# The tail rows of four batches through the second channel product: two plain products, or one pair by the seven-product method

## The chip, the cores and the metric

The kernel runs on one core of one Trainium2 chip. The metric is the time of one execution in microseconds (us). A core has several engines, each with a program of its own that it works through in order: TensorE (PE) multiplies matrices, VectorE (DVE), ScalarE (ACT) and GpSimd (POOL) do the elementwise work, SyncE (SP) issues transfers (DMAs). They wait for one another by semaphores. PE reads its operands from the on-chip memory and writes its results into eight banks of 128 x 512 f32; the other engines read the results there.

## The reference

Eight batches of 576 rows. First an attention without softmax, then a normalization of each head, then a block with a product over the rows (token mix) and two products over the 512 features (channel products):

```python
kv  = np.einsum('bhsd,bhse->bhde', k, v)          # 8 heads of 64
out = np.einsum('bhsd,bhde->bhse', q, kv)
rms = np.sqrt(np.mean(out * out, axis=-1, keepdims=True) + 1e-06)
x   = out / rms * g_norm                           # -> [8, 576, 512]

a1  = alpha1 * x + beta1
tok = np.einsum('ts,bsd->btd', w_tok, a1)
u   = x + lam * tok
a2  = alpha2 * u + beta2
ch  = np.maximum(a2 @ w_ch1, 0.0) @ w_ch2          # 512 -> 2048 -> 512
return u + lam * ch
```

## The kernel before

**Tiles.** The 576 rows of a batch are four blocks of 128 (c = 0 to 3) and a tail of 64. The tails of two batches (0 and 1, 2 and 3, 4 and 5, 6 and 7) share one block of 128 rows. `xm` holds the rows of a batch, `xt` the tails; x, then u, then the result stand in the same place there. `xt` has two slots, for two pairs of batches in turn.

**Stages of a batch.** kv (L638, L644, f32 matmuls), the product with q and its norm (L729 on PE, L696 to L717 on ACT, DVE and POOL), the token mix (L812, for tails L857) with its add on DVE (L822), a cast to bf16 on POOL (L900) and a transposing DMA on SP (L913) into `a2m` (`a2l` for tails). Then the first channel product: L1090 with 16 blocks of 128 of the 2048 features, four matmuls of 512 columns each; for tails L1104, 128 columns (130 in batch 1, where two columns more give a bias, L1115). ACT applies the ReLU and writes `ht` for the four blocks, `hl` for the tails (L1112 for batches 0 and 1, L1121 later).

**Second channel product.** For batches 0 and 1 it is plain (`ch2`, L1151): 16 matmuls of 512 columns for each block of rows, and once more 16 for the tails of both (c = 4). From batch 2 on `strassen(b)` takes the four blocks as a 2 x 2 matrix of blocks, and the weights too (B11, B12, B21, B22), and forms the result from seven products (`product`, L1212, matmuls of 256 columns) in place of eight. It needs sums of blocks: of the weights once (`weight_sums`), of the activations per batch (`sums` ahead of the products, `sums_late` between them), all in `both` on DVE (L1174). Three products stay apart: ACT copies each (`keep`, L1242) and POOL adds it to the result (L1245). The other four results are added by DVE (`last_add`, L1250). SP stores them (L1263).

**The tails of batches 2 to 7.** Those of 2 and 3 go through `ch2_tail`: 16 matmuls for the left 256 columns (L1306), and 16 for the right half (L1312) against a sum that DVE makes in between; `finish` adds (L1327) and stores them (L1346). The tails of 4 to 7 are two blocks of 128 rows and go through the seven-product method as a pair, `strassen(NB)`, at the end of the program, after batches 6 and 7 (whose first channel products are formed together, L1031 and L972).

**What sets the order.** The code makes a list of operations with their reads and writes. `ORDER` is a string written out by hand with their numbers in the order in which every engine meets them; `:n` names the bank, `+` weaves the matmuls of two operations one by one, `~n` puts in n idle matmuls. `GATES` makes single operations wait for others. Semaphore waits follow from reads, writes and gates. POOL also issues the loads of K and V (L1465 the large ones, L1469 the 64 tail rows), SP the loads of q (L1457), all in the place where `ORDER` has them. A load of q is turned by DVE (L1475).

Of the kernel before, what the change touches and what calls it, by code (L numbers as in the profile page):

```python
# [13 lines left out]
NB = 8  # L14
# [344 lines left out]
def bass_transnormer_attn__then__resmlp_affine_kernel(  # L359
# [15 lines left out]
    with ExitStack() as stack:  # L375
# [843 lines left out]
        def strassen(b):  # L1219
# [58 lines left out]
            if tails:  # L1278
                store(0, fl)
# [343 lines left out]
```

## Time and profile before

| | us |
|---|---|
| median of 3 runs | 327.81 (327.43 to 328.18) |
| profiled execution | 328.12 |
| its span, first to last instruction | 326.3 |
| PE busy | 319.0 (98%) |
| DVE busy | 250.2 (77%) |
| ACT busy | 177.1 (54%) |
| POOL busy | 141.9 (43%) |

The span starts with the first instruction of the profiled execution, and all places in time are counted from there. In rows of a timeline the first number is the start, the second how long one instruction or a series took; `[... <-X]` is the time that the engine stood idle before it, and what released it. In rows by groups `| busy, mean ns of one | idle before, releaser`. A row of the chain of waits is the start, the length, and what worked. In tables by stage each row has a stretch, its length, the busy time of PE, PE's weight loads, DVE, ACT and POOL with the number of instructions in brackets, the granted clock, the DMA share and GB/s. DMA issues end with the time from issue to landing. Names of tiles are without their numbers: `w` is `w1` or `w2`, `ps` a result bank, `hh` the buffer that holds `ht` and `hl`.

### The profile page before, as it was taken

To read this page: it belongs to the slowest core of one execution; us is meant where nothing else is said; L and a number is where in the kernel's file an instruction comes from. 1 tells how busy PE (TensorE), PEld (TensorE's weight loads), DVE (VectorE), ACT (ScalarE), POOL (GpSimd) and SP (SyncE) were. 2 spreads that over 40 slices of the span, in tenths; PEclk is the share of its full clock that TensorE was granted. 3 is DMA by queue.
4 is the path that set the end of the run, shared out by engine and by line. 5 is a ranking of instruction groups with operands and counts; after the bars stand their busy time and mean duration, and the time that the engine had idled before them with its cause. 6 is when DMAs were issued, how large, how long until landed. Compare 5 with 4: busy or idle time off the path is not lost.

```text
span 326.3 us, 6145 instructions
## 1 busy us (share of the span) xinstructions
PE 319.0 (98%) x2411; PEld 218.2 (67%) x2441; DVE 250.2 (77%) x459; ACT 177.1 (54%) x363; POOL 141.9 (43%) x147
## 2 busy tenths in 40 slices
PE   8989999999999999999999999999999999999996
PEld 7767664454766545786579874787657644589884
DVE  4586078667799997838985388889899899997672
ACT  5684572329633471738741876731883068765520
POOL 3699127798362562353337143455234600014041
PEclk9999999999999999999999999999999999999999
DMA  7999997999950994799449950998040340000116
GB/s 258 316 267 257 214 243 176 224 151 209 265 123 16 204 245 70 173 247 217 104 50 186 259 104 11 213 253 171 2 129 2 64 145 4 0 2 2 64 50 209
DMA packets 108532, 48.15 MB, mean 148 GB/s; under 512 B 82061, under 2 KB 101717, under 8 KB 108504
## 3 DMA queue, kind: packets, MB, share of 16 engines
q0 software_dynamic: 26800, 21.38, 33.4%
q1 hardware_dynamic: 72240, 25.06, 33.4%
q10 hardware_dynamic: 9464, 1.32, 2.5%
q8 instruction: 19, 0.31, 0.4%
q14 instruction: 9, 0.07, 0.1%
HBM read 38.82 MB, written 9.44 MB: 148 GB/s over the span
## 4 chain that ended last, share of the span: by engine, by line
PE 91%; DMA 3%; DVE 2%; ACT 1%; issue 1%; POOL 0%; ACTq 0%; SPq 0%
PE ps L1090 25%; PE ps L1212 25%; PE ps L1151 10%; PE ps L812 9%; PE ps L1031 7%; PE ps L729 3%; DMA hh<-in_moe_w_tok_dram 2%; PE ps L638 2%; PE ps L1104 2%; PE ps L972 2%; PE ps L857 1%; DMA xm<-in_q_dram 1%; PE ps L594 1%; PE ps L644 1%; PE ps L877 1%
## 5 line engine op out<-in xcount | busy, mean ns | idle before, releaser
L1090 PE MATMUL ps<-a2m,w 128*128 128x512 bf16 x370 | 96.1, 384 | 0.5 <-DMA a2m<-a2b 0.3
L717 POOL TENSOR_TENSOR rm<-xm,la_bc 128x512 bf16<-128x512 f32 x28 | 35.3, 1272 | 60.7 <-DVE xm L714 43.6
L1090 PEld LDWEIGHTS ps<-a2m,w 128*128 128x128 bf16 x384 | 36.2, 97 | 37.4 <-DMA a2m<-a2b 0.5
L919 ACT ACTIVATE hh<-ps,b 128x512 bf16<-128x512 f32 x72 | 47.5, 687 | 18.6 <-PE ps L1090 13.3
L1245 POOL TENSOR_TENSOR xm<-xm,tmp 128x512 f32<-128x512 f32 x18 | 22.8, 1270 | 63.5 <-DVE qp L1174 28.6
L729 PE MATMUL ps<-kvc,qt 128*128 128x128 f32 (+1 forms) x140 | 42.3, 403 | 0.1
L1212 PE MATMUL ps<-w,hh 128*128 128x256 bf16 x344 | 41.8, 273 | 0.1
L1212 PEld LDWEIGHTS ps<-w,hh 128*128 128x128 bf16 x344 | 33.4, 98 | 6.1 <-issue 0.4
L1151 PE MATMUL ps<-w,hh 128*128 128x512 bf16 x138 | 36.9, 385 | 0.1
L638 PE MATMUL ps<-vr,kr 128*128 128x128 f32 x112 | 34.7, 409 | 0.0
L699 DVE TENSOR_REDUCE small<-sq 128x8 f32<-128x512 f32 (+1 forms) x35 | 23.4, 675 | 11.7 <-ACT sq L696 11.6
L812 PE MATMUL ps<-rm,wt 128*128 128x512 bf16 x107 | 29.0, 381 | 0.3 <-DVE rtl L712 0.2
L1250 DVE TENSOR_TENSOR xm<-ps,xm 128x512 f32<-128x512 f32 x24 | 16.3, 687 | 16.5 <-POOL xm L1245 8.9
L729 PEld LDWEIGHTS ps<-kvc,qt 128*128 128x128 f32 (+1 forms) x140 | 27.2, 195 | 2.3 <-DVE kvc L657 0.7
L900 POOL CAST a2b<-xm 128x512 bf16<-128x512 f32 x24 | 14.3, 612 | 32.6 <-DVE xm L822 20.1
L1478 ACT ACTIVATE qt<-qp 128x576 fp32r<-128x576 f32 x24 | 16.0, 680 | 16.0 <-DVE qp L1475 16.0
L707 DVE TENSOR_TENSOR ps<-ps,small 128x512 f32<-128x512 f32 (+1 forms) x35 | 24.2, 694 | 0.6
L1242 ACT ACTIVATE tmp<-ps 128x512 f32<-128x512 f32 (+1 forms) x21 | 11.8, 566 | 23.5 <-PE ps L1212 23.4
L696 ACT ACTIVATE sq<-ps 128x512 f32<-128x512 f32 (+1 forms) x35 | 20.6, 596 | 6.7 <-PE ps L729 6.3
L919 ACT ACTIVATE hh<-ps 128x512 bf16<-128x512 f32 x32 | 17.5, 596 | 12.1 <-issue 7.4
L638 PEld LDWEIGHTS ps<-vr,kr 128*128 128x128 f32 x112 | 22.4, 200 | 1.5
L1151 PEld LDWEIGHTS ps<-w,hh 128*128 128x128 bf16 x144 | 13.4, 97 | 13.5 <-issue 0.4
(216 smaller groups left out, 616.8 us busy)
## 6 DMA issues: line engine op xcount, KB each, us to landing
out_dram<-xm SPq DMA_DIRECT2D x32, 256.0 KB, 2.4
kr<-in_k_dram POOLq DMA_DIRECT2D x7, 1024.0 KB, 8.0
vr<-in_v_dram POOLq DMA_DIRECT2D x7, 1024.0 KB, 8.2
qs<-in_q_dram SPq DMA_DIRECT2D x20, 288.0 KB, 4.4
w<-in_moe_w_ch_dram POOLq DMA_DIRECT2D x8, 512.0 KB, 10.9
xm<-in_q_dram SPq DMA_DIRECT2D x8, 288.0 KB, 5.8
qs<-in_v_dram SPq DMA_DIRECT2D x4, 288.0 KB, 5.7
w<-in_k_dram SPq DMA_DIRECT2D x4, 288.0 KB, 5.6
```

The costliest lines, as they stand in the source:

```text
L638: P.mm("fill", 128, [lambda e, t=t, c=c, h=h, o=128 * (h % 4): e.matmul(t.ap()[:, o:o + 128], kr4[:, h, c:c + 2, :].rearrange("p c d -> p ...
L699: P.op("DVE", dve(n), lambda e: e.tensor_reduce(out=st, in_=sq[rs, s3, 0:nst, :], axis=AX.X, op=ALU.add), r=[("sq", s3)], w=[("sm", s4)])
L707: P.op("DVE", dve(n), lambda e: e.tensor_tensor(out=grp(ps()), in0=grp(ps()), in1=st[..., None].to_broadcast([rs.stop - rs.start, nst, DH] ...
L717: P.op("POOL", pool(n), lambda e: e.tensor_tensor(out=r, in0=x.rearrange("p h e -> p (h e)"), in1=la, op=ALU.mult), r=xks + ["la"], w=rks)
L729: P.mm("fill", 128, [lambda e, p=p: e.matmul(dst(p), qt[:, p, cs], kvc[:, i, p, :], start=(p == 0), stop=(p == 3)) for p in range(4)], r=[ ...
L812: P.mm("fill", 512, [lambda e, sc=sc: e.matmul(t.ap(), wt[:, sc if sc < 4 else tw(b), 128 * c:128 * c + 128], rsrc(b, sc, al), start=(sc = ...
L919: P.op("ACT", act(512, 0 if f is None else 1), lambda e: e.activation(dst, t.ap(), ACT.Relu, bias=0.0 if f is None else b1[:, f:f + 1]), r ...
L1031: P.mm("main", 512, [lambda e, i=i: e.matmul(t.ap(), lhs[:, i, 128 * x + o:128 * x + o + 128], rhs[:, i, :], start=(first and i == 0), sto ...
L1090: P.mm("main", 512, [lambda e, dj=dj: e.matmul(t.ap(), w1[:, dj, 128 * fj:128 * fj + 128], a2m[:, b % 2, dj, :], start=(dj == 0), stop=(dj ...
L1151: P.mm("main", 512, [lambda e, fj=fj, t=t, c=c: e.matmul(t.ap(), (ht[:, fj, 128 * c:128 * c + 128] if c < 4 else hl[:, fj, :]), w2[:, fj, ...
L1212: P.mm("main", 256, [lambda e, c=c, fj=fj: e.matmul(t.ap()[:, 256 * c:256 * c + 256], at[:, fj, 128 * c:128 * c + 128], rhs(fj), start=(fi ...
L1245: P.op("POOL", pool(256 * n), lambda e, cs=cs, f=f: e.tensor_tensor(out=X[:, cs, f], in0=X[:, cs, f], in1=two(tmp[:, s]), op=ALU.add), r=x ...
```

## The change

The tails of batches 0 to 3 are now two blocks of 128 rows that go through the seven-product method as a pair, `strassen(NB + 1)`, after `strassen(3)`. For that the tails of batches 0 and 1 are kept longer: `xt` has three slots, and their ReLU results go to `hl3`, which is made of two tiles whose use is over by then (`lam_bc`, 8 blocks, and `a1f`, 8 blocks). c = 4 of `ch2(1)` and the whole of `ch2_tail` are gone. The results of these tails are stored in halves of 256 columns, eight stores where there were four of 512. `ORDER` and `GATES` are written anew; of the operations that stay, many stand in another place, among them the four transposing DMAs of batch 2, in the order of blocks 0, 1, 2, 3 (before 1, 2, 3, 0).

```diff
-        xt = sb("xt", [128, 2, DM], F32)
+        xt = sb("xt", [128, 3, DM], F32)
+        hl3 = [x.bitcast(BF16).rearrange("p (j t) -> p j t", j=8) for x in (lam_bc[:], a1f[:, 0])]
...
+        def xs(b):
+            return b // 2 % 3
+
         def xv(b, c):
-            return xm[:, b % 4, c, :] if c < 4 else xt[part(b, c), (b // 2) % 2, :]
+            return xm[:, b % 4, c, :] if c < 4 else xt[part(b, c), xs(b), :]
...
                 P.op("ACT", act(128 * n), lambda e: e.activation(
-                    hl[:, f4:f4 + n, :], v()[:, :, 0:128], ACT.Relu), r=[t],
-                    w=[("hl", f4 + j) for j in range(n)])
+                    hl3[f4 // 8][:, f4 % 8:f4 % 8 + n, :], v()[:, :, 0:128], ACT.Relu), r=[t],
+                    w=[("hl3", f4 + j) for j in range(n)])
...
-            for f4 in range(0, 16, 3 if b == 1 else 4):
-                ch1_tail(b, f4, min(3, 16 - f4) if b == 1 else 4)
+            for f4 in (0, 3, 6, 8, 11, 14) if b == 1 else range(0, 16, 4):
+                ch1_tail(b, f4, (3, 3, 2)[f4 % 8 // 3] if b == 1 else 4)
...
         def blocks(b):
             if b == NB:
                 return hl[:, 0:8], hl2[:, 0:8], hl[:, 8:16], hl2[:, 8:16]
+            if b > NB:
+                return hl3[0], hl[:, 0:8], hl3[1], hl[:, 8:16]
...
-            tails, n = b == NB, 1 if b == NB else 2
+            tails, n = b >= NB, 1 if b >= NB else 2
+            row = {xs(i): i for i in ((4, 6) if b == NB else (0, 2))}
...
-                        bb = 4 + 2 * c + i
-                        P.dma("ACT" if c and i else "SP", "oz" if c and i else "ot%d%d" % (c, i),
+                        bb = row[c] + i
+                        z = bb == NB - 1
+                        P.dma("ACT" if z else "SP", "oz" if z else "ot%d%d" % (c, i),
...
-        def ch2_tail(b):
...
+            if b == 1:
+                alias([("hl3", f) for f in range(8)], ["lam"])
+                alias([("hl3", f) for f in range(8, 16)], [("a1f", 0)])
...
             if b < 2:
-                cs = (0, 1, 2, 4, 3) if b else (0, 1, 2, 3)
-                ch2(b, [(c, n) for c in cs for n in range(4)] if b else
-                    [(c, n) for n in range(4) for c in cs])
+                ch2(b, [(c, n) for c in range(4) for n in range(4)] if b else
+                    [(c, n) for n in range(4) for c in range(4)])
             else:
                 strassen(b)
-                if b % 2 and b < NB - 3:
-                    ch2_tail(b)
+                if b == 3:
+                    strassen(NB + 1)
```

The order moves at three places. The first is PE after the products of batch 3, between the first channel products and norms of batch 5; `w2` are the weights, `hh` the ReLU results, `kvc` and `qt` operands of the norm. Before, the tails of batches 2 and 3:

```order
L1306 MATMUL ps<-w2,hh 128x256 x8
L729 MATMUL ps<-kvc,qt 128x2x64
L1090 MATMUL ps<-a2m,w1 128x512
...
L1306 MATMUL ps<-w2,hh 128x256 x8
L729 MATMUL ps<-kvc,qt 128x2x64
...
L1312 MATMUL ps<-w2,hh 128x256 x16
```

Now, the pair (`a1f` and `lam_bc` hold the ReLU results of batches 0 and 1, `hs` the sums, `ws2`, `ab_bc` and `ws1` sums of weights):

```order
L1219 MATMUL ps<-w2,a1f 128x256 x4
L1219 MATMUL ps<-ws2,hs 128x256 x8
L1219 MATMUL ps<-ab_bc,lam_bc 128x256 x8
L1219 MATMUL ps<-w2,hh 128x256 x8
L1096 MATMUL ps<-a2m,w1 128x512 x4
L735 MATMUL ps<-kvc,qt 128x2x64
L1219 MATMUL ps<-w2,a1f 128x256 x2
L735 MATMUL ps<-kvc,qt 128x2x64
...
L735 MATMUL ps<-kvc,qt 128x2x64
L1219 MATMUL ps<-ws1,hh 128x256 x2
```

Ahead of these stand the first half of one product with `a1f`, eight tail matmuls of batch 3, the product of `w2` with `lam_bc` and eight norm matmuls woven with first channel products of 512 columns; twelve norm matmuls are now woven with two matmuls of 256 columns each, which before stood between matmuls of 512.

The second place is the stretch before batch 2's first channel product (L1090, now L1096). PE before, from the last tokens' norm on:

```order
L729 MATMUL ps<-kvc,qt 128x2x64
L1151 MATMUL ps<-w2,hh 128x512 x13
L1090 MATMUL ps<-a2m,w1 128x512 x44
L638 MATMUL ps<-vr,kr 128x128
L1090 MATMUL ps<-a2m,w1 128x512
```

and now:

```order
L735 MATMUL ps<-kvc,qt 128x2x64
L1157 MATMUL ps<-w2,hh 128x512
L1096 MATMUL ps<-a2m,w1 128x512 x44
L641 MATMUL ps<-vr,kr 128x128
L1096 MATMUL ps<-a2m,w1 128x512
```

The run of 13 is one now; ahead of it, since the last token product of batch 2, stand 15 others in both cases, woven with norm matmuls, and 12 of batch 1's tail matmuls (before 16). On POOL, which issues the loads of K and V of batch 4 there (`vr`, `kr`), before:

```order
L717 TENSOR_TENSOR rm<-xm,la_bc 128x512 x4
L900 CAST a2b<-xm 128x512 x4
L1469 DMA vr<-in_v_dram 64x8x64
L1465 DMA vr<-in_v_dram 128x8x256
L1465 DMA kr<-in_k_dram 128x8x256
L1469 DMA kr<-in_k_dram 64x8x64
L717 TENSOR_TENSOR rm<-xm,la_bc 128x512 x4
```

and now:

```order
L723 TENSOR_TENSOR rm<-xm,la_bc 128x512 x2
L906 CAST a2b<-xm 128x512 x4
L1447 DMA kr<-in_k_dram 128x8x256
L1447 DMA vr<-in_v_dram 128x8x256
L723 TENSOR_TENSOR rm<-xm,la_bc 128x512
L1451 DMA vr<-in_v_dram 64x8x64
L1451 DMA kr<-in_k_dram 64x8x64
L723 TENSOR_TENSOR rm<-xm,la_bc 128x512 x3
```

The large loads go first, K ahead of V, and the small ones behind a norm's product of batch 3.

The third place is SP, around the stores of these tails and the loads of batch 6's q. Before:

```order
L1263 DMA out_0_dram<-xm 128x512
L1457 DMA qs<-in_q_dram 32x72x32
L1346 DMA out_0_dram<-xt 64x512
L1457 DMA qs<-in_q_dram 32x72x32
L1346 DMA out_0_dram<-xt 64x512
L913 DMA_TRANSPOSE a2m<-a2b 128x4x128
```

and now:

```order
L1268 DMA out_0_dram<-xt 64x256
L1439 DMA qs<-in_q_dram 32x72x32
L1268 DMA out_0_dram<-xt 64x256 x2
L1439 DMA qs<-in_q_dram 32x72x32
L1272 DMA out_0_dram<-xm 128x512
L1268 DMA out_0_dram<-xt 64x256
L1439 DMA qs<-in_q_dram 32x72x32
L1272 DMA out_0_dram<-xm 128x512
L1268 DMA out_0_dram<-xt 64x256 x3
L919 DMA_TRANSPOSE a2m<-a2b 128x4x128 x4
L1268 DMA out_0_dram<-xt 64x256
```

Before, one store of tails stood ahead of the last load of q; now four do.

More of the change, by code (lines that the diff above doesn't have):

```diff
@@ L1168, in four @@
             js = range(8 * m + 4 * g, 8 * m + 4 * g + 4)
-            if b == NB:
-                return [("hl%d" % n if n else "hl", fj) for fj in js]
+            if b >= NB:
+                return [(("hl", "hl1", "hl3", "hl")[2 * (b - NB) + n], fj) for fj in js]
             return [(hkey(b), fj, n) for fj in js]
@@ L1177, in hsv @@
         def hsv(b):
-            return hs[:, :, 0:128] if b == NB else hs
+            return hs[:, :, 0:128] if b >= NB else hs
         def t1(fj):
@@ L1234, in xks @@
                 if tails:
-                    return [xk(4 + 2 * cs.start + i, 4, p) for i in range(2)
+                    return [xk(row[cs.start] + i, 4, p) for i in range(2)
                             for p in range(f.start // 128, f.stop // 128)]
@@ L1266, in strassen @@
             fl, fh, up, dn = slice(0, 256), slice(256, 512), slice(0, n), slice(n, 2 * n)
+            if tails:
+                up, dn = (slice(i, i + 1) for i in row)
             ta, tb, tc = (P.bank("main") for _ in range(3))
@@ L1278, in strassen @@
             if tails:
-                store(0, fl)
+                store(up.start, fl)
             product(ta, False, hsv(b), lambda j: ws2[:, j, :], lambda g: [("hs", g), ("t2", g)], False)
@@ L1287, in strassen @@
             if tails:
-                store(1, fh)
+                store(dn.start, fh)
             product(tc, False, A12, lambda j: B22[:, j, :],
@@ L1291, in strassen @@
             last_add(tc, up, fh)
-            for c in range(n):
+            for c in range(up.start, up.stop):
                 store(c, fh)
@@ L1296, in strassen @@
             last_add(ta, dn, fl)
-            for c in range(n, 2 * n):
+            for c in range(dn.start, dn.stop):
                 store(c, fl)
-        def ch2_tail(b):
-            hk = [("hl", fj) for fj in range(16)]
-            t = P.bank("main")
-            for n in range(4):
-                P.mm("main", 256, [lambda e, fj=fj: e.matmul(
-                    t.ap()[:, 0:256], hl[:, fj, :], w2[:, fj, 0:256], start=(fj == 0),
-                    stop=False) for fj in range(4 * n, 4 * n + 4)],
-                    r=[("w2", n)] + hk[4 * n:4 * n + 4], w=[t])
-            both(ALU.add, hl[:, 8:16], hl[:, 8:16], hl[:, 0:8], hk[0:8], hk[8:16])
-            for n in range(4):
-                P.mm("main", 256, [lambda e, fj=fj: e.matmul(
-                    t.ap()[:, 256:512], hl[:, fj, :], w2[:, fj, 256:512],
-                    start=False, stop=(fj == 15)) for fj in range(4 * n, 4 * n + 4)],
-                    r=[("w2", n)] + hk[4 * n:4 * n + 4], w=[t])
-            finish(b, 4, t)
         def finish(b, c, t):
@@ L1320, in finish @@
             pp = range(a // 128, z // 128)
-            if c < 4:
-                x, ks = xm[:, b % 4, c, a:z], [xk(b, c, p) for p in pp]
-            else:
-                x = xt[:, (b // 2) % 2, a:z]
-                ks = [xk(bb, 4, p) for bb in (b - 1, b) for p in pp]
+            x, ks = xm[:, b % 4, c, a:z], [xk(b, c, p) for p in pp]
             if b:
@@ L1338, in finish @@
                     r=ks + [("tmp", s)], w=ks, pri=-1000)
-            if c < 4:
-                P.dma("SP", "o%d%d" % (b % 4, c), dcost(128, 86.0 * (z - a) / DM),
-                      lambda e: e.dma_start(out[b, 128 * c:128 * c + 128, a:z], x), r=ks)
-            else:
-                for i in range(2):
-                    P.dma("SP", "ot%d%d" % ((b // 2) % 2, i),
-                          dcost(64, 86), lambda e, i=i:
-                          e.dma_start(out[b - 1 + i, 512:576, a:z], x[64 * i:64 * i + 64, :]),
-                          r=ks[len(pp) * i:len(pp) * i + len(pp)])
+            P.dma("SP", "o%d%d" % (b % 4, c), dcost(128, 86.0 * (z - a) / DM),
+                  lambda e: e.dma_start(out[b, 128 * c:128 * c + 128, a:z], x), r=ks)
         wtt = P.bank("any")
```

11 lines of the change are left out of this document (5 added, 6 removed), and 140 rows, old and new, of tables (GATES, ORDER).

## The prediction

> **What bounds the kernel now.** I read the page first (the engines' busy time and the shares of the chain that ended last), then TensorE's waits, then the pieces of the chain, and last the tables by stage and the timelines of two places.
>
> ```profile
> span 326.3 us, 6145 instructions
> PE 319.0 (98%) x2411; PEld 218.2 (67%) x2441; DVE 250.2 (77%) x459; ACT 177.1 (54%) x363; POOL 141.9 (43%) x147
> PE 91%; DMA 3%; DVE 2%; ACT 1%; issue 1%; POOL 0%; ACTq 0%; SPq 0%
> ```
>
> TensorE is busy for 98% of the span and carries 91% of the chain. What little it waits is listed by its waits:
>
> ```profile
> PE ps L465 <- DVE fil L464: 1.1, 1, 1.1
> ...
> PE ps L1090 <- DMA a2m<-a2b: 0.3, 1, 0.3
> PE ps L812 <- DVE rtl L712: 0.2, 1, 0.2
> ```
>
> L465 is in the kernel's opening, which the change leaves alone; 0.5 us belong to the two waits in the stages that are reordered. So the time is TensorE's instruction stream, and the first question is how long the removed and the added matmuls occupy it. The chain gives that, start to start:
>
> ```profile
> 51.79 3.45 PE ps L1151 x16
> ...
> 182.63 0.87 PE ps L1306 x8
> ...
> 184.67 0.87 PE ps L1306 x8
> ...
> 186.72 1.75 PE ps L1312 x16
> ...
> 311.00 12.06 PE ps L1212 x108
> 323.08 0.42 DVE xt L1250
> ```
>
> A matmul with 512 columns takes 3.45 / 16 = 0.216 us, one with 256 columns 0.87 / 8 = 0.109 us. The last row is the end: a DVE add of the last product and its stores, which both kernels share.
>
> **Matmuls removed and added.** Before, the tails of batches 0 and 1 are 16 matmuls of 512 columns (3.45 us), those of batches 2 and 3 are 8 + 8 + 16 of 256 columns (0.87 + 0.87 + 1.75 = 3.49 us): 6.94 us. Now seven products of 8 matmuls with 256 columns do both: 56 x 0.109 = 6.10 us. The difference is **-0.84 us**, on the engine that sets the end. The tails of batches 0 and 1 leave the first channel product in six groups as before (of 3, 3, 2, 3, 3, 2 blocks for 3, 3, 3, 3, 3, 1), with as many matmuls.
>
> **Norm matmuls beside shorter ones.** Twelve f32 norm matmuls (line 729) that stood between channel products of 512 columns now stand between pairs of the new products of 256.
>
> ```profile
> 184.51 1.04 PE L1306 MATMUL ps<-w,hh 128*128 128x256 bf16 x8
> 185.30 0.31 PE L729 MATMUL ps<-kvc,qt 128*128 128x128 f32 x1
> 185.45 0.39 PE L1090 MATMUL ps<-a2m,w 128*128 128x512 bf16 x1
> 185.49 0.41 PE L729 MATMUL ps<-kvc,qt 128*128 128x128 f32 x1
> 185.75 0.39 PE L1090 MATMUL ps<-a2m,w 128*128 128x512 bf16 x1
> ```
>
> In the steady pattern one channel product starts 0.30 us after the last (185.45, 185.75), 0.08 more than the 0.216 without a norm matmul. Behind eight matmuls of 256 columns the last of these starts at 184.51 + 7 x 0.109 = 185.27 and the next channel product at 185.45: 0.18, or 0.07 more than 0.109. No row shows the pattern 256, 256, f32, 256. If it costs 0.07 the twelve gain 0.1 us; if the f32 matmul takes its whole own step (0.15, 185.30 to 185.45), they lose 12 x 0.07 = 0.8 us. The row nearest in kind is the 0.07 behind a 256-column product, so I take **-0.1 us** and keep +0.8 for the range.
>
> **Work on the other engines.** The pair has eight sums of 128x512 and four last adds of 128x256 on DVE, three copies on ACT and three adds on POOL; the old tails had two adds of 128x512 and one of 128x1024.
>
> ```profile
> L1174 DVE TENSOR_TENSOR hh<-hh,hs 128x512 bf16<-128x512 bf16 x2 | 0.8, 424 | 0.1
> L1250 DVE TENSOR_TENSOR xt<-ps,xt 128x256 f32<-128x256 f32 x4 | 1.7, 423 | 1.7 <-POOL xt L1245 1.0 <-PE ps L1212 0.6
> L1327 DVE TENSOR_TENSOR xt<-ps,xt 128x512 f32<-128x512 f32 x2 | 1.3, 660 | 0.0
> L1174 DVE TENSOR_TENSOR hh<-hh 128x1024 bf16<-128x1024 bf16 x11 | 7.5, 681 | 0.0
> L1242 ACT ACTIVATE tmp<-ps 128x256 f32<-128x256 f32 x3 | 1.1, 382 | 6.5 <-PE ps L1212 6.5
> L1245 POOL TENSOR_TENSOR xt<-xt,tmp 128x256 f32<-128x256 f32 x3 | 2.2, 742 | 4.0 <-ACT tmp L1242 4.0
> ```
>
> DVE: 12 x 0.42 - 2 x 0.66 - 0.68 = +3.0 us; ACT +1.1; POOL +2.2. All of it falls behind batch 3's channel products, where the tables by stage show room:
>
> ```profile
> 80.00:100.00 20.00, 19.95 (x153) 13.37 (x155) 16.30 (x33) 10.90 (x25) 8.35 (x6) 1.00 0.77 172
> 100.00:120.00 20.00, 19.95 (x117) 11.04 (x117) 19.68 (x39) 10.14 (x21) 10.44 (x12) 1.00 0.85 169
> 180.00:190.00 10.00, 10.00 (x105) 8.51 (x105) 5.15 (x10) 7.00 (x21) 2.54 (x2) 1.00 1.08 233
> ```
>
> (Busy us of TensorE, its weight loads, DVE, ACT, POOL; then the granted clock, 1.00.) In 180 to 190 us DVE works 5.15 of 10. I take **0** for the 3.0 us; without that cover they would cost up to their full length. One chain can show: the pair's third and fourth product need sums of the last ReLU rows, and between the last of batch 3's tail matmuls and the fourth product's second half TensorE has by the new order 24 x 0.109 + 8 x 0.30, about 5.0 us. On DVE six sums, one norm reduce (0.68, line 699's kind) and one last add stand there: 7 x 0.42 + 0.68 = 3.6 us, and an ACT ReLU ahead. Bounds 0 and, if the norm chain puts three more DVE instructions of 0.7 in front, about +0.5; I take +0.1.
>
> **The stretch that loses TensorE work.** The 16 tail matmuls of batches 0 and 1 do not leave the program where the new ones come in. They leave before batch 2's first channel product (line 1090 at 111.86):
>
> ```profile
> 109.04 2.98 PE L1151 MATMUL ps<-w,hh 128*128 128x512 bf16 x12
> 111.86 9.66 PE L1090 MATMUL ps<-a2m,w 128*128 128x512 bf16 x43
> 121.17 0.41 PE L638 MATMUL ps<-vr,kr 128*128 128x128 f32 x1
> ```
>
> By the order, between the last token matmul and 111.86 there were 28 of 512 columns, 15 norm matmuls and 16 of the tail; now 16, 16 and 12: 12 x 0.216 + 4 x 0.056 - 0.08, about 2.7 us less (0.056 is half of 0.109 for 128 columns, an estimate). What 111.86 and 121.17 wait for therefore has 2.7 us less cover:
>
> ```profile
> L913 SPq DMA_TRANSPOSE a2m<-a2b x4: 1206/1262/1267, 103.6 to 107.5; - x4
> DMA to landing us min/median/max: 2.4/2.5/3.5
> ...
> 107.62 0.73 POOL L1469 DMA_DIRECT2D vr<-in_v_dram  x1 [2.26 <-DMA a2m<-a2b]
> ...
> L1465 POOL DMA_DIRECT2D kr<-in_k_dram x1: 1421/1421/1421, 109.2 to 109.2; - x1
> DMA to landing us min/median/max: 6.6/8.3/9.9
> ```
>
> The last of the four transposes is in by 107.5 + 3.5 = 111.0 at the latest, 0.9 us ahead of its use. The large K load is in by 109.2 + 9.9 = 119.1, 2.1 us ahead. Taken alone, 2.7 us less would make TensorE wait 1.8 us for the transpose. Against it the new order sets three things: the remaining 0.7 us of the 3.45 goes before the token matmuls, which brings these forward; the first block's transpose goes first, whose cast follows the first add, instead of fourth; and the small V load (0.73) goes behind the large ones. The transposes can end up to one issue (1.26) plus that 0.7 earlier, which leaves 1.8 - 2.0, about nothing, and the K load 0.7 + 0.7 earlier, which leaves 2.1 + 1.4 - 2.7 = 0.8 of slack. So this place costs from 0 to 1.8 us; I take **+0.3**, nearer the low end since all three steps stand in the order.
>
> **Waits of before.** The new order moves batch 5's transposes and the last token product's operands, on which the 0.5 us above depends. Bounds -0.5 and 0; I take -0.2.
>
> **Sum:** -0.84 - 0.1 + 0.1 + 0.3 - 0.2 = -0.74, about **-0.7 us**. The profiled execution took 328.12 us (1.8 around its span), 0.3 above the median of 327.81; the forecast is the median less 0.7, **327.1 us**.
>
> **The rivals.** *One, slower:* in 100 to 120 us DVE is busy 19.68 of 20 and the transposes keep their times. Then TensorE only moves its idle time: 1.8 us of wait ahead of batch 2's channel product, and -0.84 - 0.1 + 1.8 = +0.9, or 328.7 us. It decides from the point where TensorE waits more than 0.9 us in this stretch. For it: DVE loses there only one add (0.66), so what runs through it hardly gets earlier. Against it: DVE is idle 3.7 us in 80 to 100, and the order of the transposes.
>
> *Two, no change by SP:* half rows make eight stores of four, each waiting for a last add and standing among batch 6's q loads on a queue in order.
>
> ```profile
> 189.71 0.49 SPq L1346 DMA_DIRECT2D out_dram<-xt  x1
> 190.66 0.32 SPq L1457 DMA_DIRECT2D qs<-in_q_dram  x1
> ...
> 196.86 1.44 DVE L1475 STREAM_TRANSPOSE qp<-qs 128x576 f32<-128x576 f32 x2
> ...
> qs<-in_q_dram SPq DMA_DIRECT2D x20, 288.0 KB, 4.4
> ```
>
> The last q load, issued at 190.66, lands by the median about 195.1, 1.8 us ahead of the DVE transpose. Two last adds later plus two more issues (0.42 + 0.42 + 2 x 0.49, 1.8 us) just use that up; DVE then waits, and with it the norm of batch 6. One more step of the kind costs 0.9 us: 328.0 us. Against it: by the order, DVE has fourteen other instructions between the add and that transpose.
>
> *Three, more gain:* nothing waits in the stretch and the 0.5 us go whole: -0.84 - 0.1 - 0.5 = -1.4, or 326.4 us.
>
> *Four, locked DVE and POOL.* One row shows a sum held up while POOL adds:
>
> ```profile
> 170.92 1.26 POOL L1245 TENSOR_TENSOR xm<-xm,tmp 128x512 f32<-128x512 f32 x1 [3.88 <-DVE hh L1174]
> ...
> 171.59 1.14 DVE L1174 TENSOR_TENSOR hh<-hs,hh 128x1024 bf16<-128x1024 bf16 x1
> ```
>
> 1.14 us against 0.68 for its group. The pair brings eight such sums and three POOL adds of 0.74. If each add held up one sum, and each of these stood before a waiting product, 3 x 0.45 = 1.3 us would be added to -0.7: 328.4 us, still within what counts as no change. I give this little, since most sums of that shape show their group's plain length. [...]
>
> **How the numbers follow.** A difference under 0.2% (0.66 us) cannot be told from none here. The forecast's case has 0.55: with its unknown terms from -0.4 to +0.4 around -0.7 it falls 0.33 below 327.15 and 0.20 within, 0.02 above. More gain: 0.13, faster. The slower rival: 0.15, of it 0.13 above 328.47. SP: 0.12, within. The lock: 0.05, within. So faster 0.46, same 0.39, slower 0.15. The range is 326.2 (all gains with nothing lost, and 0.2 for the spread) to 328.5 us, which leaves out most of the slower rival and hardly anything else.
>
> **What would show it.** Right: TensorE busy shorter by about 0.9 us, no wait of it over 0.3 us between 100 and 125 us, the new products of 256 columns 0.109 us apart, 0.28 for two of them with a norm matmul. Wrong: a wait of line 1096 (the channel product's new number) on the DMA transposes or of the K/V products on a load near 109 and 119 us; TensorE waiting at the pair's third or fourth product for DVE; the stream transposes of batch 6 on DVE waiting for a q load; or steps of 0.3 us and more in the woven pattern.

## The result: slower by 0.6%, and the profile after

The changed kernel takes 330.7 us (median of 18 runs, 328.23 to 336.0) against 327.87 us (18 runs, 327.22 to 329.04) for the kernel before on the same chip: a ratio of 1.0063, 95% interval 1.0043 to 1.0083. Four of the 18 runs (333.16 to 336.0 us, the profiled one among them) are more than 1.5% above the fastest, with a mean granted clock of 0.990 to 0.995; the ratio leaves them out, the median does not. The forecast was 327.1 us with a range up to 328.5; it was wrong in sign.

The page of the changed kernel, first its span, its busy times, and the shares of the chain that ended last:

```profile
span 332.1 us, 6186 instructions
PE 321.9 (97%) x2418; PEld 220.5 (66%) x2449; DVE 256.5 (77%) x468; ACT 179.2 (54%) x366; POOL 146.3 (44%) x150
PE 87%; DVE 7%; ACT 2%; DMA 2%; issue 1%; SPq 0%
```

TensorE now has 87% of the chain where it had 91%, and the view of its waits has one that was not there:

```profile
PE ps L735 <- issue: 3.2, 1, 3.2
PE ps L468 <- DVE fil L467: 1.1, 1, 1.1
...
PE ps L641 <- issue: 0.3, 1, 0.3
PE ps L735 <- DVE b L1121: 0.2, 1, 0.2
```

TensorE's timeline shows where it stands. First the stretch before and in batch 2's first channel product, then batch 3's first channel product:

```profile
107.39 0.33 PE L735 MATMUL ps<-kvc,qt 128*128 128x128 f32 x1 [0.21 <-DVE b L1121]
108.65 9.77 PE L1096 MATMUL ps<-a2m,w 128*128 128x512 bf16 x43
118.67 0.30 PE L641 MATMUL ps<-vr,kr 128*128 128x128 f32 x1 [0.25 <-issue]
...
139.85 0.30 PE L735 MATMUL ps<-kvc,qt 128*128 128x128 f32 x1
143.37 0.66 PE L735 MATMUL ps<-kvc,qt 128*128 128x128 f32 x1 [3.22 <-issue]
143.84 0.65 PE L1096 MATMUL ps<-a2m,w 128*128 128x512 bf16 x1
```

In the kernel before, the same place shows no gap, and the wait column of the last rows is empty:

```profile
142.33 0.79 PE L729 MATMUL ps<-kvc,qt 128*128 128x128 f32 x2
142.96 0.39 PE L1090 MATMUL ps<-a2m,w 128*128 128x512 bf16 x1
```

The second of the two norm matmuls in the first row starts at 142.71, as a narrower window shows:

```profile
142.71 0.41 PE L729 MATMUL ps<-kvc,qt 128*128 128x128 f32 x1
```

So TensorE came to the norm matmul ahead of batch 3's first channel product at 139.85 instead of 142.33, that is 2.5 us earlier, and stood until 143.37, 0.7 us later than the 142.71 of before. The matmuls behind the wait are also longer (0.65 against 0.39). The table of the changed kernel by stretches of 2 us says why: its granted clock fell.

```profile
140.00:142.00 2.00, 0.15 (x2) 0.01 (x1) 0.69 (x1) 0.00 (x0) 0.00 (x0) 1.00 1.34 307
142.00:144.00 2.00, 0.63 (x3) 0.49 (x4) 0.00 (x0) 0.00 (x0) 0.00 (x0) 0.61 2.25 233
144.00:146.00 2.00, 2.00 (x9) 1.18 (x8) 0.00 (x0) 0.60 (x1) 0.00 (x0) 0.50 1.04 145
146.00:148.00 2.00, 2.00 (x12) 1.52 (x9) 0.65 (x2) 0.00 (x0) 0.00 (x0) 0.50 0.81 130
148.00:150.00 2.00, 2.00 (x12) 1.29 (x12) 1.56 (x5) 1.17 (x3) 0.00 (x0) 0.68 1.18 188
150.00:152.00 2.00, 2.00 (x19) 1.59 (x17) 1.10 (x2) 0.98 (x3) 1.26 (x1) 1.00 1.14 230
```

The channel products behind the wait start 0.56 us apart (143.84, 144.40) where those of before start 0.29 apart (142.96, 143.25). An estimate from the table: the missing clock costs 2 x 0.50 + 2 x 0.50 + 2 x 0.32 = 2.6 us, and 0.3 more for 143.4 to 144. In narrower stretches the clock is 1.00 for 142.0 to 142.4 and 0.50 for 142.8 to 143.4, and at the other end 0.50 for 148 to 149 and 1.00 for 149.3 to 149.6. So it went to 0.50 at about 142.4, 2.3 us into the wait, and was back at 1.00 from 149.3, 5.9 us after the work began again. What sets these two times is not shown. In two experiments below a wait of 5.2 us went with a clock of 0.50 and one of 1.75 us with 1.00.

What the wait is for is read from the four transposes of batch 3, `a2m`, and from the loads that POOL issues between them. The view of the line gives issue times and the times from issue to landing, here of the changed kernel, with POOL's timeline behind it:

```profile
L919 SPq DMA_TRANSPOSE a2m<-a2b x4: 1197/1268/3790, 127.7 to 131.6; - x4
DMA to landing us min/median/max: 2.4/5.1/11.7
```

```profile
130.42 0.95 POOL L1447 DMA_DIRECT2D vr<-in_v_dram  x1 [1.62 <-DMA a2m<-a2b]
...
132.03 0.90 POOL L1447 DMA_DIRECT2D kr<-in_k_dram  x1
```

and the same of the kernel before:

```profile
L913 SPq DMA_TRANSPOSE a2m<-a2b x4: 1190/1266/2070, 129.2 to 134.5; - x4
DMA to landing us min/median/max: 3.3/4.2/8.2
```

```profile
133.40 0.95 POOL L1465 DMA_DIRECT2D vr<-in_v_dram  x1 [1.00 <-DMA a2m<-a2b]
...
135.02 0.90 POOL L1465 DMA_DIRECT2D kr<-in_k_dram  x1
```

The last transpose is issued 2.9 us earlier than before (131.6 against 134.5), but the two loads of 1 MB for batch 5 are issued 3.0 us earlier as well, one ahead of the last transpose and one behind it as before, and the slowest transpose takes 11.7 us instead of 8.2. It lands at 131.6 + 11.7 = 143.3, 0.1 us ahead of the start at 143.37; before at 134.5 + 8.2 = 142.7, where the next matmul starts at 142.71. So the transfer had nothing to spare in the kernel before, and the whole lead of TensorE was lost to it. Why it took 3.5 us longer in the same company is not shown; what it takes without the loads is shown by e1 below.

### The profile page after: what moved, and what is told of

It reads as the page before. It is cut to its first block, busy times and chain, and to the rows that moved or that the text cites. A ratio compares the mean times of both kernels' runs of the same rounds, so it can differ in the third digit from the quotient of the medians.

```text
span 332.1 us, 6186 instructions
## 1 busy us (share of the span) xinstructions
PE 321.9 (97%) x2418; PEld 220.5 (66%) x2449; DVE 256.5 (77%) x468; ACT 179.2 (54%) x366; POOL 146.3 (44%) x150
## 4 chain that ended last, share of the span: by engine, by line
PE 87%; DVE 7%; ACT 2%; DMA 2%; issue 1%; SPq 0%
PE ps L1219 26%; PE ps L1096 25%; PE ps L818 8%; PE ps L1157 7%; PE ps L1037 7%; PE ps L735 3%; PE ps L641 2%; PE ps L978 2%; PE ps L1110 2%; DMA w<-in_k_dram 2%; PE ps L863 1%; DVE w L1138 1%; DVE small L786 1%; DVE xm L828 1%; PE ps L619 1%
## 5 line engine op out<-in xcount | busy, mean ns | idle before, releaser
L1096 PE MATMUL ps<-a2m,w 128*128 128x512 bf16 x368 | 97.6, 389 | 0.4
L1096 PEld LDWEIGHTS ps<-a2m,w 128*128 128x128 bf16 x384 | 36.6, 98 | 40.3 <-issue 4.5
L735 PE MATMUL ps<-kvc,qt 128*128 128x128 f32 (+1 forms) x140 | 44.5, 409 | 3.4 <-issue 3.2
L1219 PE MATMUL ps<-w,hh 128*128 128x256 bf16 x352 | 44.2, 276 | 0.0
L1219 PEld LDWEIGHTS ps<-w,hh 128*128 128x128 bf16 x352 | 34.2, 99 | 7.1 <-issue 1.1
L1157 PE MATMUL ps<-w,hh 128*128 128x512 bf16 x123 | 33.5, 386 | 0.0
L906 POOL CAST a2b<-xm 128x512 bf16<-128x512 f32 x24 | 16.7, 711 | 33.3 <-DVE xm L828 23.9
L735 PEld LDWEIGHTS ps<-kvc,qt 128*128 128x128 f32 (+1 forms) x140 | 28.1, 201 | 2.9 <-DVE b L1121 0.5
L1250 ACT ACTIVATE tmp<-ps 128x512 f32<-128x512 f32 (+1 forms) x24 | 12.9, 544 | 22.1 <-PE ps L1219 22.1
L1157 PEld LDWEIGHTS ps<-w,hh 128*128 128x128 bf16 x128 | 11.9, 97 | 11.7 <-issue 0.4
```

Source lines behind the costliest of these rows:

```text
L735: P.mm("fill", 128, [lambda e, p=p: e.matmul(dst(p), qt[:, p, cs], kvc[:, i, p, :], start=(p == 0), stop=(p == 3)) for p in range(4)], r=[ ...
L1096: P.mm("main", 512, [lambda e, dj=dj: e.matmul(t.ap(), w1[:, dj, 128 * fj:128 * fj + 128], a2m[:, b % 2, dj, :], start=(dj == 0), stop=(dj ...
L1157: P.mm("main", 512, [lambda e, fj=fj, t=t, c=c: e.matmul(t.ap(), ht[:, fj, 128 * c:128 * c + 128], w2[:, fj, :], start=(fj == 0), stop=(fj ...
L1219: P.mm("main", 256, [lambda e, c=c, fj=fj: e.matmul(t.ap()[:, 256 * c:256 * c + 256], at[:, fj, 128 * c:128 * c + 128], rhs(fj), start=(fi ...
```

## The experiments

**Measures.** TensorE's main part is counted from the start of its first matmul of the first channel product to the start of its last matmul; what lies ahead of it took 28.6 to 30.4 us in the profiles, whatever the kernel, so single profiles are compared by the main part and kernels by their medians. By the steps of the prediction's rows the matmuls taken out and put in make 0.84 us less (16 x 0.216 against 24 x 0.109). The kernel before has one profile only, and profiles of one kernel differ too: 292.35 and 292.54 for e7 and its repetition.

| kernel | median us (runs) | ratio, 95% interval | main part | TensorE idle, 100 to 120 | wait at batch 3's channel product |
|---|---|---|---|---|---|
| before | 327.87 to 328.23 | 1 | 293.32 | 0.05 | under 0.1 |
| the change, first profile | 330.7 (18) | 1.0063 [1.0043, 1.0083] | 299.36 | 0.52 | 3.2 |
| e0_changed | 330.15 (12) | 1.0046 [1.0017, 1.0075] | 296.19 | 1.55 | 1.75 |
| e1_loads_behind | 329.63 (12) | 1.0044 [1.0023, 1.0066] | 293.85 | 0.56 | none |
| e2_before_short | 334.48 (6) | 1.0187 [1.0154, 1.0220] | 299.13 | 5.21 | 0.4 |
| e3_idle_matmuls | 331.71 (6) | 1.0109 [1.0080, 1.0138] | 296.74 | 0.61 | filled |
| e4_first_and_behind | 328.69 (12) | 1.0012 [0.9993, 1.0031] | 293.72 | 1.16 | none |
| e10_only_sums_later | 328.63 (12) | 1.0016 [0.9991, 1.0042] | 294.82 | 0.00 | 1.6 |
| e7_sums_later | 327.20 (12) | 0.9961 [0.9941, 0.9981] | 292.35 | 0.00 | none |
| e7_again | 327.36 (12) | 0.9972 [0.9950, 0.9995] | 292.54 | 0.16 | none |
| e8_loads_earlier | 326.97 (12) | 0.9962 [0.9941, 0.9982] | 292.48 | 0.03 | none |
| e9_stores_later | 326.93 (12) | 0.9961 [0.9940, 0.9982] | 292.40 | 0.10 | none |
| e11_before_remedied | 328.90 (12) | 1.0017 [0.9993, 1.0042] | 293.77 | 0.00 | none |

Each ratio is against the kernel before on the same chip: one chip for e1 to e4, one for e0, e7, e8 and e9, one for e7_again, e10 and e11.

**The theory and its rivals.** The theory: the removed work is not missed where it is removed alone; TensorE runs ahead until the pair gives work back near 180 us, and whatever the other engines deliver in between with less slack than that lead becomes a wait; at batch 3's channel product it is the transposes, held up by the loads among them. Rivals: the pair itself (its sums, copies and stores) slows something; or the stretch at 100 to 120 us, as the prediction's first rival had it, carries the loss alone.

### e0_changed: the changed kernel again

No edit.

> The changed kernel itself, beside the next three on one chip: 2 to 3 us over the kernel before, 0.6 to 0.9%.

330.15 us, 2.0 us over the kernel before; the ratio of 1.0046 is under the expected 0.6 to 0.9%. The profile (330.69 us) lies near the median, and shows the plain case: a wait of 1.75 us and no loss of clock behind it (1.00 in every stretch).

```profile
119.76 0.30 PE L641 MATMUL ps<-vr,kr 128*128 128x128 f32 x1 [1.34 <-DVE rtl L718]
...
140.93 0.31 PE L735 MATMUL ps<-kvc,qt 128*128 128x128 f32 x1
142.99 0.38 PE L1096 MATMUL ps<-a2m,w 128*128 128x512 bf16 x1 [1.75 <-issue]
```

The wait at 140 and the loss around 107 and 118 us are both in it. The second is larger here than in the first profile. From batch 2's first channel product (108.65) to the first K/V product it is 11.11 us, against 10.02 in the first profile and 121.17 - 111.86 = 9.31 before; and TensorE starts 0.3 us late at 107.39, where a reduction on DVE (line 1121) stands behind the scaling of `w1`. So this stretch costs 1.0 to 2.1 us. The accounts nearly close: in this profile 2.1 + 1.75 - 0.84, less the 0.5 of waits before, is +2.5 of the 296.19 - 293.32 = 2.9 us by which the main part grew; in the first 1.0 + 3.2 + 2.9 - 0.84 - 0.5 = +5.8 of 299.36 - 293.32 = 6.0. The 0.2 to 0.4 us left over are not traced.

### e2_before_short: the kernel before with TensorE work taken away

```diff
-                    w2[:, fj, :], start=(fj == 0), stop=(fj == 15))
-                    for fj in range(4 * n, 4 * n + 4)],
+                    w2[:, fj, :], start=(fj == 0), stop=(n == 3 and fj == (12 if b and c == 3 else 15)))
+                    for fj in range(4 * n, 4 * n + (1 if b and ((c == 3 and n) or (c == 4 and n == 0)) else 4))],
```

It leaves out twelve matmuls of 512 columns of batch 1's second channel product (2.6 us), so block 3 and the tails of batches 0 and 1 lack parts of their sums. Nothing of the pair is in it.

> The kernel before with 12 matmuls of 512 columns left out of batch 1's second channel product (9 of block 3, 3 of the tail; these rows come out incomplete), ahead of batch 2's first channel product, nothing else changed. It removes 2.6 us of TensorE work where the change removes it, without the pair. Theory (cover lost in front of batch 3's transposes, whose landing follows the loads): TensorE waits 1.5 to 2.6 us near 140 us, and the time falls only by 0 to 1.1 us: 326.7 to 327.8. Rival (the time is TensorE's stream): 327.8 - 2.6 = 325.2.

2.6 us less work made the kernel 6.3 us slower (334.48 against 328.17 on the same chip, ratio 1.0187). The place was not the expected one: the wait came at batch 2's channel product, 5.2 us long.

```profile
115.82 6.52 PE L1090 MATMUL ps<-a2m,w 128*128 128x512 bf16 x22 [5.21 <-DVE xm L714]
```

```profile
L913 SPq DMA_TRANSPOSE a2m<-a2b x4: 1189/1232/1267, 104.3 to 109.0; - x4
DMA to landing us min/median/max: 2.4/2.9/6.5
```

The fourth transpose of batch 2 was issued at 109.0, among batch 4's loads, and landed 6.5 us later, at 115.5. The DVE instruction that the row names had merely ended last: the DVE work that this product needs, the scaling of `w1`, was done by 112.6.

```profile
111.87 0.74 DVE L1132 TENSOR_SCALAR w<-w,ab 128x2048 bf16<-128x2048 bf16 x1
```

So of the 5.2 us some 2 would have been waited for DVE in any case, and the rest is the transpose's. Before, the same four landed within 3.5 us. Then the clock, again in stretches of 2 us:

```profile
114.00:116.00 2.00, 0.18 (x1) 0.27 (x3) 1.97 (x5) 0.00 (x0) 0.00 (x0) 0.91 1.39 333
116.00:118.00 2.00, 2.00 (x6) 0.63 (x5) 1.18 (x3) 0.66 (x1) 1.44 (x2) 0.50 1.65 344
118.00:120.00 2.00, 2.00 (x8) 0.79 (x7) 0.00 (x0) 0.96 (x3) 1.04 (x1) 0.73 1.73 249
```

This shows the same course without the pair, though at another place: 2.6 us less work on the engine that bounds, a transpose crossed by loads (6.5 us to landing), a wait (5.2 us), and a clock of 0.50 behind it. So such a loss does not need the pair; that the pair adds none of its own is shown by e7 below.

### e3_idle_matmuls: the lead given back

```diff
-... 709 707 708 744:2+800:0 743 ...
+... 709 707 708 ~52 744:2+800:0 743 ...
```

52 idle matmuls of 128 columns (2.9 us by the step) ahead of batch 3's first channel product. A few lines of code, not shown, let them also wait for the last readers of the bank that they write.

> The changed kernel with 52 idle matmuls of 128 columns (2.9 us) in front of batch 3's first channel product, where TensorE waits 3.2 us. Theory: they fill the wait, so the usual time stays at 330.4 (+-0.4), and since TensorE is not idle any more the granted clock stays at 1.00 in every run and the runs above 331.5 go. If nothing really waits there, the time rises by 2.9 us to 333.3. If the clock falls for another reason, runs above 331.5 stay.

No wait is left there and the clock stays at 1.00 in the profile from 130 to 170 us, but the time is 331.71 (1.0109), above the expected 330.4, and five of the six runs are above the 331.5 that none was to pass. Against the change's ratios of 1.0046 and 1.0063 the 2.9 us of idle matmuls cost 1.5 to 2.1 us, so 0.8 to 1.4 us of them fell into time in which TensorE would have stood. The fill is the same in every run, while the wait it replaces varies (1.75 and 3.2 in the two profiles of the change). That TensorE waits there is borne out; what for, this run does not say.

### e1_loads_behind: batch 5's loads after the last transpose

```diff
-GATES = {23: 52, 38: 67, 39: 73, 40: 163, 124: 151, 125: 213, 204: 196, 233: 269, 234: 216, 235:
+GATES = {738: 638, 23: 52, 38: 67, 39: 73, 40: 163, 124: 151, 125: 213, 204: 196, 233: 269, 234: 216, 235:
```

The V load of batch 5, and the K load behind it, wait for batch 3's last transpose.

> The changed kernel with one more dependency: the loads of batch 5's K and V start behind the landing of the last of batch 3's four transposes, not of the first one. Theory (transposes crossed by these loads land too late for batch 3's first channel product): the last transpose lands near 134 us instead of 143, TensorE's wait of 3.2 us near 140 goes, the granted clock stays at 1.00, and the time is 3.2 us under the changed kernel's usual 330.4: 327.0 to 327.4. If the later loads are then late for batch 5's K/V product (used near 147 us), it gives back up to 1 us: 328. Rival (the loss lies in the pair itself, its sums, its adds or the woven norms): no change, 330.4.

```profile
L919 SPq DMA_TRANSPOSE a2m<-a2b x4: 1197/1268/1793, 128.4 to 132.2; - x4
DMA to landing us min/median/max: 2.4/2.9/4.2
```

Uncrossed, the slowest transpose takes 4.2 us, so all are in by 136.4 at the latest, and the wait at 140 is gone from the profile: its cause is the loads. The time did not follow: it is 329.63 (1.0044 [1.0023, 1.0066]) where 327.0 to 327.4 was expected, and cannot be told from the change's 1.0046 and 1.0063. In the profile, that of a run somewhat under the median, the main part is 293.85, 2.3 under that of e0, and still 0.5 above before. What is left stands in two places: the stretch up to 120 us (0.3 at 107 and 10.06 us for the 9.31 up to the K/V product), and 0.46 us of idle in 140 to 160, where POOL, which now issues the V load at 135.8 (5.4 us later than in the first profile), does its adds behind the loads.

### e4_first_and_behind: the first block's transpose ahead as well

```diff
-... 628 646 625 679:7 722+631:5 ... 731 634 630 626 637 639:6 ...
+... 628 646 625 626 679:7 722+631:5 ... 731 634 630 637 639:6 ...
```

To the gate of e1 it adds: SP issues the transpose of batch 3's block 0 (626) right behind its cast (625).

> As the run with the later loads, and SP issues the transpose of batch 3's block 0 first (its cast is ready at 125.0 us, it was third). Theory: all four transposes land by 133, the loads start at about 133 as in the kernel before, no wait of TensorE near 140 and none for batch 5's K/V: 327.0 us. Rival (loss in the pair): 330.4.

328.69 us, 1.0012 [0.9993, 1.0031]: no difference from before can be told, and the interval lies below the 1.0043 to 1.0083 of the change, though it overlaps that of e0 (1.0017 to 1.0075). Nothing waits from 140 to 160 us, and the expected 327.0 is missed by what is left in 100 to 120: 1.16 us of idle. The profile names DVE for its largest wait there,

```profile
119.94 0.30 PE L640 MATMUL ps<-vr,kr 128*128 128x128 f32 x1 [0.89 <-DVE ps L712]
```

but the large V load of batch 4 ends there. POOL issued it at 108.38 and it landed 11.5 us later, at 119.9. The same holds in e0 (107.74 + 11.9 = 119.6 for a start at 119.76) and in the first profile of the change:

```profile
L1447 POOL DMA_DIRECT2D vr<-in_v_dram x1: 976/976/976, 107.7 to 107.7; - x1
DMA to landing us min/median/max: 10.8/10.8/10.8
```

107.7 + 10.8 = 118.5 for a start at 118.67. In the new order V goes behind K, so V is the one that lands last.

### e10_only_sums_later: room on DVE in 100 to 120 us, nothing at 140

```diff
-... 571 515 647 522 ... 452 455 648 445 ... 613 617 649 576 ... 683 650 644 624 ...
+... 571 515 522 ... 452 455 445 ... 613 617 576 ... 683 644 647 624 ... 628 646 648 625 ... 677:4 632 650 684 ... 730 728 649 731 ...
-    260, 237: 298, 371: 465, 399: 275, 448: 647, 452: 647, 456: 648, 460: 648, 466: 465, 468:
-    467, 579: 578, 580: 578, 581: 578, 582: 578, 590: 533, 606: 649, 614: 649, 625: 646, 629:
+    260, 237: 298, 371: 465, 399: 275, 466: 465, 468:
+    467, 579: 578, 580: 578, 581: 578, 582: 578, 590: 533, 625: 646, 629:
```

Three sums of weights (647, 648, 649; 0.69 us each on DVE), which stood between 99 and 116 us, go behind batch 3's norm, with a fourth (650) that stood at 120.3; the gates that made batch 2's casts and batch 3's norm wait for them go.

> The changed kernel with only the second remedy: three weight sums moved from 99 to 116 us to behind 120 us on DVE (and the gates on casts taken away), but batch 3's transposes and batch 5's loads as the change has them. Theory: the 1.5 to 2.5 us lost between 105 and 120 us go, TensorE then comes so much earlier to batch 3's first channel product, where the transposes land as before, near 142 to 143 us: the wait there grows by as much, the time stays at 330 to 331, and with a longer wait the granted clock falls more often. If the two losses are independent, 328 to 328.7.

The loss around 107 and 118 us is gone, and the wait at 140 stays:

```profile
100.00:120.00 20.00, 20.00 (x119) 11.32 (x117) 18.57 (x36) 13.19 (x27) 10.81 (x12) 1.00 0.81 186
```

```profile
141.36 0.38 PE L1095 MATMUL ps<-a2m,w 128*128 128x512 bf16 x1 [1.58 <-DVE xm L1257]
```

328.63 us, 1.0016. The expectation that the recovered time would only lengthen the wait at 140 (330 to 331 us) missed; the two places added up as independent ones. This is no proof that they always would: the last transpose was issued later (132.8) and still landed no later than 132.8 + 8.5 = 141.3. Such landings vary by 3 us between profiles of nearly the same order (8.5 us here, 11.7 in the first profile).

How the sums brought the V load in is only partly shown. With them gone the casts of batch 2 take 0.61 us each; with them there the last one meets the scaling of `w1` and takes 1.67, as POOL's timeline of e0 has it, and the two scalings it meets differ in length:

```profile
104.26 1.67 POOL L906 CAST a2b<-xm 128x512 bf16<-128x512 f32 x1 [0.58 <-DVE xm L828]
106.50 1.25 POOL L1447 DMA_DIRECT2D kr<-in_k_dram  x1 [0.58 <-DMA a2m<-a2b]
107.74 0.97 POOL L1447 DMA_DIRECT2D vr<-in_v_dram  x1
```

```profile
104.71 0.73 DVE L1138 TENSOR_SCALAR w<-w,ab 128x2048 bf16<-128x2048 bf16 x1
105.49 0.98 DVE L1138 TENSOR_SCALAR w<-w,ab 128x2048 bf16<-128x2048 bf16 x1
```

The V load is issued 0.15 us earlier in e10 (107.59) and lands after 10.4 us instead of 10.8 to 11.9. What makes that difference stays open.

### e7_sums_later: both remedies

The edits of e4 and of e10 together.

> As the run with block 0's transpose first and the later loads of batch 5 (which came to 0.12% over the kernel before), and three weight sums of 0.7 us (the second half's) on DVE go from 99 to 116 us to behind batch 3's norm, after 120 us, with the gates that hung casts on them taken away. Theory (DVE, busy without a gap there, holds back the w1 scaling, the casts and so batch 2's first channel product; the lost 16 tail matmuls had covered it): TensorE loses 0.5 to 0.8 us less between 105 and 112 us, 327.4 to 327.8 where the kernel before has 327.9. If the K/V loads of batch 4 decide at 118 us anyway, the wait only moves there: no change against that run.

327.20 us, 0.9961 [0.9941, 0.9981]: faster than the kernel before, a little under the 327.4 to 327.8 expected, and 2.95 us faster than the change (330.15) on the same chip. Its page, and of the waits of TensorE that are left, all in the kernel's opening, the longest two:

```profile
span 325.3 us, 6218 instructions
PE 318.9 (98%) x2449; PEld 218.4 (67%) x2449; DVE 255.6 (79%) x468; ACT 178.8 (55%) x366; POOL 145.4 (45%) x150
PE 91%; DMA 3%; DVE 2%; ACT 1%; ACTq 0%; issue 0%; POOL 0%; SPq 0%
```

```profile
PE ps L467 <- DVE fil L466: 1.1, 1, 1.1
PE ps L1338 <- DMA hh<-in_moe_w_tok_dram: 0.5, 1, 0.5
```

The main part is 292.35, 0.97 under before, and in the repetition (e7_again) 0.78 under; the matmul steps alone make 0.84. The 0.5 us of waits of before are gone too and do not show on top, which stays open. So the gain of the change, when nothing takes it back, is about 1 us. Its woven norms, the pattern that the prediction had no row for:

```profile
188.93 0.39 PE L1218 MATMUL ps<-ws,hh 128*128 128x256 bf16 x2
189.08 0.30 PE L734 MATMUL ps<-kvc,qt 128*128 128x128 f32 x1
...
189.52 0.40 PE L1218 MATMUL ps<-ws,hh 128*128 128x256 bf16 x2
```

Two products of 256 columns and one norm matmul take (189.52 - 188.93) / 2 = 0.295 us (the rows left out are another two and one), so the norm adds 0.295 - 2 x 0.109 = 0.077, as beside 512 columns (0.08).

### e8_loads_earlier and e9_stores_later: more slack for batch 4's loads

```diff
+        for i in (575, 576, 577, 578):
+            self.ops[i].deps.discard(self.ops[457])
+            self.ops[i].deps.add(self.ops[453])
```

e8 is e7 with batch 4's K and V loads released by the transpose of block 1 and not of block 2.

> As the last, and batch 4's K and V loads are released by the second of batch 2's transposes, not the third (1.3 us earlier). Theory: the wait of 0.3 to 1.0 us for them ahead of batch 4's K/V product goes too: 326.9 to 327.3, against 327.9 before. Rival: the transposes that these loads now cross come later by as much, and batch 2's first channel product waits: no gain over the last.

e9 is e8 with two stores of batch 1 behind the q loads on SP:

```diff
-... 719:2+673:1 621 557 551 582 580 581 579 720+623:6 ...
+... 719:2+673:1 621 582 580 581 579 557 551 720+623:6 ...
```

> As the last, and SP issues two of batch 1's stores (256 KB each) behind batch 4's q loads, so that they do not share the DMA engines with the K and V loads. If these stores slow the loads, another 0.2 to 0.5 us; else no change.

326.97 and 326.93, ratios 0.9962 and 0.9961: no difference from e7 (0.9961), so the 0.2 to 0.5 us more that e9 might have brought are not there. With 0.00 to 0.10 us of TensorE idle left in 100 to 120 us, the earlier transfers were worth nothing.

### e11_before_remedied and e7_again: whose gain is it

e11 does to the kernel before what e7 does to the change: its sums of weights (654 to 657) go behind batch 3's norm, their gates go, block 0's transpose (633) goes ahead, and batch 5's loads (745 on) wait for the last transpose (637).

```diff
-... 579 581 454:4 654 451 ... 522:6 527:5 655 523 ... 660:1 662:6 656 619 ... 675 673 657 628 ... 641 564 633 643 ...
+... 579 581 454:4 451 ... 522:6 527:5 523 ... 660:1 662:6 619 ... 675 673 628 ... 690 654 653 ... 635 691 657 655 652 ... 632 633 636 ... 735 656 647 ...
-GATES = {23: 52,
+GATES = {745: 637, 23: 52,
```

> The kernel before with the same remedies (three weight sums later and their gates off, block 0 of batch 3 transposed first, batch 5's loads behind the last transpose). It loses only about 0.5 us of TensorE time between 100 and 180 us, so the theory expects 0 to 0.4 us less than before. If the remedies and not the pair made the gain of 1.1 us, it gains as much: 1 us and more.

> The changed kernel with both remedies once more, beside these two: 0.9 to 1.3 us under the kernel before (0.996 to 0.997).

The remedies alone bring nothing, 328.90 us, 1.0017 [0.9993, 1.0042]; e7 on the same chip is again faster, 327.36, 0.9972 [0.9950, 0.9995]. So the gain of e7 needs the pair. e11 is not an exact counterpart, though: its sums now stand among DVE's adds of the token mix, and TensorE stands 0.17 us at 128.81 for such an add (line 820), which it does not in the kernel before, so part of what the remedies save may be lost again there.

## Why the prediction was wrong

- **Matmuls removed and added (-0.84): right.** e7, where nothing else intervenes, is 0.97 and 0.78 under before in the main part. The sign that was to show it, a busy TensorE shorter by 0.9 us, is on no page (318.9 in e7 against 319.0): the page of before counts 2411 matmuls, that of e7 2449, so busy times of two pages do not compare to a microsecond.
- **Norm matmuls beside shorter ones (-0.1): about nothing.** The surcharge is 0.077 beside 256 columns and was 0.08 beside 512; inside the bounds.
- **Work on the other engines (0, and 0.1 for the pair's chain): right.** From 170 to 200 us TensorE is busy for 29.95 to 30.00 of 30 in every profile of the pair; the rivals on SP's stores and on DVE's sums held up by the pair's adds on POOL show nowhere in TensorE's waits.
- **Waits of before (-0.2): right in sign**; both waits, 0.3 and 0.2, are gone in the change.
- **The stretch that loses TensorE work (+0.3): mis-sized.** It cost 1.0 and 2.1 us in the two profiles of the change. The step named 2.7 us less cover and the lines that would wait, but it followed the K load, "0.8 of slack", where the new order issues V behind K: V is the load that lands last, after 10.8 to 11.9 us, which takes up the 1.4 us of earlier issue. The transposes did not wait at all (batch 2's first channel product starts at 108.65 with no gap), so the slower rival had the sign and the stretch, and its 1.8 us of wait is within what the stretch cost, but it named another transfer; its +0.9 for the whole kernel falls short by what the next step lost.
- **The step that was missing, and that decided.** The prediction checked the 2.7 us against the deadlines up to 121 us and stopped. The lead lasts until the pair gives the work back near 180 us, so all deliveries between had to be checked, and batch 3's transposes had no slack in the trace of before (landed by 142.7, with the next matmul at 142.71), which the prediction did not count, that is, put at nothing. TensorE waited 1.75 to 3.2 us there, and where the wait was 3.2 us it lost some 2.9 us more at half the clock. So the change loses 1.5 and 2.1 us by its two ratios (1.0046 and 1.0063), where its matmuls alone gain 0.84.

That the transposes were held up by loads is shown by e1 (gated: 4.2 us and no wait) and e2 (crossed without the pair: 6.5 us). That the two places together make the loss is shown by e7, which removes both; what each is worth in time is known less well, since e1 alone gained nothing that can be told, e4 and e10 about 1 us each. That the sums on DVE are behind the late V load is shown as a whole by e10; the link between them is not.

## What to carry to other kernels

When work leaves the engine that bounds the kernel, that engine runs ahead until the place where work comes back: list each delivery of the other engines on that way with its slack (last landing against first use), and compare every one with the lead. A transfer that others need soon can come late among large loads that nobody needs yet: here the slowest of batch 3's transposes took 8.2 to 11.7 us to landing among them and 4.2 behind a gate. The gate on the loads took the whole wait out of the profile, and together with an earlier transpose it brought the ratio from 1.0046 to 1.0012. And a wait can cost more than itself: in the one profile with a wait of 3.2 us, a clock of 0.50 behind it took another 2.9 us by the estimate above.

## What the hardware showed that was not expected

- A transpose of 128x512 bf16 lands 2.4 to 4.2 us after its issue where batch 5's loads of 1 MB wait for the last of the four (e1, e7); where such loads from another queue went out ahead of the last one or with it, the slowest of four takes 6.5 (e2), 8.2 (before), 8.5 (e10) and 11.7 us (first profile of the change). How the loads delay it is not shown.
- The granted clock fell to 0.50 at waits of 3.2 and 5.2 us, 2.3 us into the first of them and some 5.0 into the second, and stayed at 1.00 at waits of 1.6 and 1.75. It was back at 1.00 5.9 and some 3.3 us after the work began again. (The two times in e2 are estimates from the means of 0.91 for 114 to 116 us and 0.73 for 118 to 120, taking 0.50 and 1.00 as the only values.)
- A cast on POOL (0.61 us) took 1.67 where it ran beside two scalings of 128x2048 bf16 on DVE. The scalings took 0.73 and 0.98; one at 107.29 that met no cast took 0.95, so the cast is not shown to have lengthened them.
- In e0 the profile names a DVE instruction (L718, 119.00 to 119.69) as the releaser of the K/V product at 119.76. In the first profile of the change that product starts at 118.67, ahead of the same instruction (119.00), so it does not need it; the V load landed at 119.6 and 118.5, 0.1 to 0.2 us ahead of the product in both. The name was not the cause here.
